# A recurrent-attention and SoLU kernel: an earlier opening, and two output banks copied out by ScalarE with the down products in another order

## The chip, the cores and the metric

One core of one Trainium2 chip. The metric is the device time of one execution in microseconds (us). All executions quoted are of the fast state (none is over 1.5% above the fastest of its kernel); a kernel is quoted by its median and by the spread of its runs. Each profile shows one execution, which is one of the runs listed (for the kernel before a further one, of 383.67 us); its span leaves out about 1.8 us that the run's own time contains (383.67 against 381.9 for the kernel before, 381.39 against 379.6 for the changed one). A *profile* here is the record of that execution, instruction by instruction; each experiment has one, so what one profile shows is one reading.

## The reference

```python
# attention: q, k, v, alpha are (4 batches, 8 heads, 768 tokens, 48), fp32
for t in range(S):
    state = alpha[:, :, t, :, None] * state + einsum('bhd,bhe->bhde', k[:, :, t], v[:, :, t])
    y[:, :, t] = einsum('bhd,bhde->bhe', q[:, :, t], state)
x = y.transpose(0, 2, 1, 3).reshape(3072, 384)

# SoLU MLP: w_in 384 x 1024, w_out 1024 x 384, both arrive as float64
h = x @ w_in
solu = h * softmax(h)
ln = (solu - mean(solu)) / sqrt(var(solu) + 1e-6) * g_ln
out = ln @ w_out
```

## The kernel before: the parts that matter

The recurrence is done in chunks of 128 tokens: running products of alpha (VectorE scans, backward and forward), scaled queries and keys, a masked score matrix for inside the chunk, and a state for what came before. A *group* is one chunk of all four batches, 512 tokens; there are six, 0 to 5. The MLP of group g runs beside the attention of group g+1. Two stretches are written out by hand: the **opening** (attention of group 0, with the float64 weights being unpacked by VectorE in `bits`) and the **turn** from the MLP of group 0 to that of group 1.

Some names of the profile's lines: `an` is alpha as loaded, `aT` alpha transposed and its forward running products, `hT` the backward ones, `kT` the keys, `qe` and `qv` the scaled queries, `a` the scores, `sT` the masked scores, `y` what attention reads out, `o` an output bank. In the MLP, *up* is x times w_in with the result `h`, `e` is its exp, the *product* is h times e on VectorE, and *down* is the matmul with w_out; d_ff is done in eight slices, so group 0 has eight products.

```python
def masked(half, batches=range(B)):              # VectorE: scores out of their bank, times the mask
    for b in batches:
        nc.vector.tensor_tensor(out=sT[:, b, half*NP : half*NP + NP], in0=masks[half][b],
                                in1=mask..., op=mult)

def down(n, half, part=slice(0, HF)):            # TensorE: 128 tokens n, half of the 8 slices of d_ff
    if half == 0 and part.start == 0:
        d["o"] = ps_o.tile([P, 512], FP, tag="o")    # an output bank; there are two
    for f in ...: nc.tensor.matmul(d["o"][:, 0:DM+1], lhsT=u_of(g, f)..., rhs=w_out[:, f], ...)

def finish(n):                                   # layer norm's mean and scale, then the store
    nc.vector.tensor_copy(out=s[:, 0:1], in_=d["o"][:, DM:DM+1])
    ... two more small VectorE instructions ...
    if g == 0:
        o = work.tile([P, DM], FP, name="o_mean")
        nc.vector.scalar_tensor_tensor(out=o, in0=mean_sb, scalar=s[:, 0:1], in1=d["o"][:, 0:DM], ...)
    nc.gpsimd.tensor_tensor(out=r, ..., op=pow)
    nc.scalar.activation(out=o_sb, in_=o, func=Copy, scale=r)
    nc.sync.dma_start(out=out[...], in_=o_sb)

# the opening
warm(18)                                         # 18 small matmuls, each recorded as two, to wake TensorE
turned(an, ...)                                  # alpha, transposed on TensorE
for i in range(3):
    nc.scalar.copy(out=aT[...], in_=t[i]); scan_back(0, i)
...
turned(qn, ends_of(qn), t)                       # queries
warm(2, ps_a, "a1")
for i in (2, 0, 1): ...                          # queries times aT
scores(0, 0); scores(0, 1, t); read_begin()
masked(0); masked(1)
bits(0)                                          # unpacks the first part of w_in
...
# the turn
mean(0); down(0, 1); mean(1); in_range(5); in_range(6); down(1, 1)
...
scan_on(1, 2); qe = tq[2] * aT; apart()
finish(0)
... two more scans and products, qv ...
down(2, 0); scores(1, 0)
finish(1)
alpha_over(1); load(alpha, an, 2)                # ScalarE's overflow test, then the next alpha
masked(0); down(2, 1); scores(1, 1); masked(1)
finish(2); alpha_T(2); read_begin()
... down(3, 0) in two parts, with the reads of the state ...
alpha_over(2); load(alpha, an, 3)
for i in range(3): scan_back(2, i)
keys_T(2); keys(2); load(k, kn, 3)
scan_on(2, 2); scan_on(2, 0)
read_values(1); down(3, 1); finish(3)
```

Of the kernel before, what the change touches and what calls it, by code (L numbers as in the profile page):

```python
# [16 lines left out]
P = 128  # L17
# [15 lines left out]
def fast_path(ctx, tc, q, k, v, alpha, moe_w_in, moe_w_out, moe_g_ln, out):  # L33
# [150 lines left out]
    def load_v_first(slot):  # L184
        x = slots[slot].rearrange("p (n d) -> p n d", d=D)
        y = vn.rearrange("p b h d -> p (b h) d")
        xi, yi = (z.rearrange("p (n i) d -> p i n d", i=2) for z in (x, y))
        nc.sync.dma_start(out=x, in_=v[:, :, 0:P].rearrange("b h p d -> p (b h) d"))
        for i in range(2):
            nc.gpsimd.tensor_copy(out=yi[:, i, :, all_of[i]], in_=xi[:, i])  # L190

# [299 lines left out]
    def down(n, half, part=slice(0, HF)):  # L491
# [4 lines left out]
        for f in range(half * HF + part.start, half * HF + part.stop):  # L496
# [2 lines left out]
                stop=(f == FC - 1), skip_group_check=True,  # L499
            )  # L500

    def finish(n):
        g, b = divmod(n, B)
        d = st[n]
        s, o = sums[:, n], d["o"][:, 0:DM]
        t0 = b * S + g * P
        if g == G - 1:
            o_sb = work.tile([P, DM], FP, name="o_sb")
            r = gr[g]["r"][:, b : b + 1]
            nc.scalar.activation(out=o_sb, in_=o, func=AF.Copy, scale=r)  # L510
            nc.scalar.dma_start(out=out[t0 : t0 + P, :], in_=o_sb)
            d.clear()
            return
        nc.vector.tensor_copy(out=s[:, 0:1], in_=d["o"][:, DM : DM + 1])
        t = small.tile([P, 1], FP, name="t")
        nc.vector.scalar_tensor_tensor(
            out=t, in0=s[:, 0:1], scalar=-1.0 / DFF, in1=s[:, 0:1], op0=ALU.mult, op1=ALU.mult
        )
        nc.vector.tensor_tensor(out=s[:, 3:4], in0=t, in1=gr[g]["s"][:, b : b + 1], op=ALU.add)  # L519
        if g == 0:  # L520

            o = work.tile([P, DM], FP, name="o_mean")
            nc.vector.scalar_tensor_tensor(  # L523
                out=o, in0=mean_sb, scalar=s[:, 0:1], in1=d["o"][:, 0:DM], op0=ALU.mult, op1=ALU.add
            )
        r = small.tile([P, 1], FP, name="r")
        nc.gpsimd.tensor_tensor(out=r, in0=s[:, 3:4], in1=mhalf, op=ALU.pow)  # L527
        o_sb = work.tile([P, DM], FP, name="o_sb")
        nc.scalar.activation(out=o_sb, in_=o, func=AF.Copy, scale=r)  # L529
        nc.sync.dma_start(out=out[t0 : t0 + P, :], in_=o_sb)  # L530
        d.clear()
# [83 lines left out]
    def mean(half):  # L615


        m = ps_h.tile([P, 512], FP, tag="h", name="sums")[:, 0:DM]
        if half == 0:
            for f in range(FC):  # L620
                r = quarter(f % 4)
                nc.tensor.matmul(
                    m[r], lhsT=ones[:, 0:32], rhs=w_out[:, f, 0:DM], start=f < 4, stop=f >= FC - 4,
                    tile_position=(0, r.start), skip_group_check=True,
                )
            made["m"] = work.tile([P, DM], FP, name="o_mean")
            nc.scalar.mul(out=made["m"], in_=m, mul=-1.0 / (32 * DFF))
        else:
            nc.tensor.matmul(m, lhsT=ones, rhs=made["m"], start=True, stop=True)
            nc.scalar.copy(out=mean_sb, in_=m)  # L630
# [33 lines left out]
        return [pool.tile([P, NP, P], FP, tag=tag, name=f"{name}{i}") for i, (pool, tag) in enumerate(where)]  # L664


    warm(18)
    t = three("tp_a", [(ps_a, "a0"), (ps_a, "a1"), (ps_a, "a2")])
    turned(an, ends_of(an), t)
    for i in range(3):  # L670
# [8 lines left out]
        nc.vector.tensor_tensor(out=kT[:, part], in0=t[i], in1=hk[:, part], op=ALU.mult)  # L679
    scan_on(0, 0)  # L680
    t = three("tp_q", [(ps_o, "o"), (ps_o, "o"), (ps_a, "a0")])
    turned(qn, ends_of(qn), t)

    warm(2, ps_a, "a1")
    for i in (2, 0, 1):
        if i == 1:
            scan_on(0, i)
# [7 lines left out]
    t = [x.tile([P, NP, P], FP, tag=n, name="a_" + n) for x, n in ((ps_h, "h"), (ps_o, "o")) for _ in range(2)]  # L695
    scores(0, 1, t)
    read_begin()
    masked(0)
    masked(1)
    bits(0)  # L700
    read_values(0)
# [51 lines left out]
    for i in range(3):  # L753
        scan_back(1, i)
        part = slice(NP * i, NP * i + NP)
        nc.vector.tensor_tensor(out=kT[:, part], in0=tk[i], in1=hk[:, part], op=ALU.mult)
    mean(0)
    down(0, 1)
    mean(1)
    in_range(5)  # L760
    in_range(6)
    down(1, 1)
    tq += three("tp_q2", [(ps_h, "h")])
    turned(qn, ends_q, tq, range(H, NB))
    load(q, qn, 2)
    keys_back(1, three("tp", [(ps_a, "a2"), (ps_a, "a3"), (ps_h, "h")]))
    scan_on(1, 2)
    nc.vector.tensor_tensor(out=qe, in0=tq[2], in1=aT[:, H:NB, 1:SW], op=ALU.mult)
    apart()
    finish(0)  # L770
    decay(1)
    in_range(7)
    for i in range(2):
        scan_on(1, i)
        part = slice(NP * i, NP * i + NP)
        nc.vector.tensor_tensor(out=qv[:, part], in0=tq[i], in1=aT[:, part, 1:SW], op=ALU.mult)
    down(2, 0)
    scores(1, 0)
    finish(1)
    alpha_over(1)  # L780
    load(alpha, an, 2)
    masked(0)
    down(2, 1)
    scores(1, 1)
    masked(1)
    finish(2)
    alpha_T(2)
    read_begin()
    for batches, part in (((0, 1), slice(0, HF // 2)), ((2, 3), slice(HF // 2, HF))):
        down(3, 0, part)  # L790
        for n in range(len(parts)):
            read_state(n, batches)
    alpha_over(2)
    load(alpha, an, 3)
    for i in range(3):
        scan_back(2, i)
    keys_T(2)
    keys(2)
    load(k, kn, 3)
    scan_on(2, 2)  # L800
    scan_on(2, 0)
    read_values(1)
    down(3, 1)
    finish(3)


# [6 lines left out]
    )  # L813
    first = dict(
        head={3: "keys_back", 5: "masked0", 6: "masked1"},
        behind={0: "states v", 1: "on1", 2: "lasts firsts", 3: "apart", 5: "decay", 7: "alpha back"},
        tail={4: "scores0", 5: "scores1", 6: "begin read0 read1"},
        middle={7: "read2 read3 values"},
    )
# [581 lines left out]
```

## Time and profile before

| | median of 3 runs, us | lowest | highest |
|---|---|---|---|
| before | 384.48 | 383.99 | 386.02 |

The head of the page of the kernel before: busy time of each engine, its share of the span, and its instructions.

```profile
span 381.9 us, 10525 instructions
PE 367.1 (96%) x4665; PEld 221.5 (58%) x4665; DVE 245.4 (64%) x381; ACT 144.6 (38%) x258; POOL 125.0 (33%) x132
```

TensorE (PE) is busy for 96% of the span. Only the remaining 14.8 us of the span are there to be won without removing matmuls, and the prediction below shows where they lie.

### The profile page before, as it was taken

Reading aid. Unit: us, or ns where it says so; the run is one execution under the profiler, and the core shown is the slowest. Engines: PE = TensorE matmul, PEld = TensorE weight load, DVE = VectorE, ACT = ScalarE, POOL = GpSimd, SP = SyncE. Lnnn points to the kernel's source line nnn. Section 1 sums busy time; section 2 is a strip of 40 time slices with the busy share of each in tenths; the row PEclk is TensorE's granted clock in tenths of the full one; section 3 lists DMA queues with packets and bytes.
Section 4 is the critical chain, followed back from the end, with each engine's and each line's share of the span. In section 5 each row is a group of like instructions: output and inputs, shape, how many; then the busy total and the mean of one; then the engine's idle time right before and its main releaser. Section 6 shows DMA issues by size and latency. Waiting matters only on the chain.

```text
span 381.9 us, 10525 instructions
## 1 busy us (share of the span) xinstructions
PE 367.1 (96%) x4665; PEld 221.5 (58%) x4665; DVE 245.4 (64%) x381; ACT 144.6 (38%) x258; POOL 125.0 (33%) x132
## 2 busy tenths in 40 slices
PE   8889999879899999999999999999999999999995
PEld 8675355547655666555576555575555675555552
DVE  0999879996989866893565884665875411554410
ACT  2628774384526244124252225351224131233111
POOL 5010000041055990544621553630562520333210
PEclk9999999999999999999999999999999999999999
DMA  9993989304457100961000960001500000000011
GB/s 183 164 330 95 222 270 164 85 21 101 110 115 118 40 4 4 186 143 44 22 3 27 203 145 21 23 12 37 81 0 22 22 24 2 21 21 21 22 44 49
DMA packets 65510, 30.78 MB, mean 81 GB/s; under 512 B 47016, under 2 KB 63664, under 8 KB 65456
## 3 DMA queue, kind: packets, MB, share of 16 engines
q1 hardware_dynamic: 64432, 29.10, 34.4%
q10 hardware_dynamic: 1024, 0.92, 0.7%
q8 instruction: 38, 0.62, 0.7%
q14 instruction: 16, 0.13, 0.1%
HBM read 25.30 MB, written 4.72 MB: 79 GB/s over the span
## 4 chain that ended last, share of the span: by engine, by line
PE 69%; DVE 16%; ACT 6%; DMA 3%; issue 3%; SPq 2%; POOL 0%; ACTq 0%; DVEq 0%
PE o L497 28%; PE h L386 23%; PE y L312 8%; PE a L278 5%; DVE aT L219 3%; DVE room L401 2%; SPq L153 2%; DMA qn<-in_q_dram 2%; DVE hT L219 2%; DVE sT L289 1%; ACT sq L576 1%; DVE aT L194 1%; DMA an<-in_alpha_dram 1%; PE kv L361 1%; DVE top L592 1%
## 5 line engine op out<-in xcount | busy, mean ns | idle before, releaser
L497 PE MATMUL o<-w_out,room 128*128 128x385 f32 x384 | 133.7, 492 | 2.4 <-DVE o_mean L523 2.4
L386 PE MATMUL h<-x,w_in 128*128 128x512 f32 x288 | 132.2, 599 | 0.2 <-DVE g_col L613 0.2
L497 PEld LDWEIGHTS o<-w_out,room 128*128 128x128 f32 x384 | 71.5, 190 | 58.3 <-issue 16.3
L386 PEld LDWEIGHTS h<-x,w_in 128*128 128x128 f32 x288 | 53.1, 190 | 58.8 <-issue 48.5
L401 DVE TENSOR_TENSOR room<-h,e 128x512 f32<-128x512 f32 x40 | 27.6, 689 | 82.1 <-ACT e L400 82.1
L400 ACT ACTIVATE e<-h 128x512 f32<-128x512 f32 x40 | 23.9, 597 | 108.2 <-PE h L386 108.2
L527 POOL TENSOR_TENSOR r<-sums,mhalf 128x1 f32<-128x1 f32 x20 | 14.3, 713 | 137.7 <-DVE sums L519 137.7
L417 POOL TENSOR_TENSOR p<-p,e 128x512 f32<-128x512 f32 x30 | 41.8, 1392 | 15.7 <-ACT e L400 15.7
L402 ACT ACTIVATE u<-room 128x512 f32<-128x512 f32 x40 | 25.2, 630 | 35.1 <-DVE room L401 35.1
L289 DVE TENSOR_TENSOR sT<-a,mask 128x512 f32<-128x512 f32 x44 | 27.3, 683 | 9.2 <-PE a L278 9.0
L219 DVE TENSOR_TENSOR_SCAN hT<-aT,unit 128x516 f32<-128x516 f32 x18 | 23.2, 1355 | 8.3 <-ACT aT L671 8.3
L240 POOL TENSOR_TENSOR kT<-kT,hT 128x1024 f32<-128x1024 f32 (+1 forms) x8 | 14.2, 1798 | 42.9 <-DVE kT L194 42.9
L219 DVE TENSOR_TENSOR_SCAN aT<-aT,seed 128x516 f32<-128x516 f32 x18 | 27.2, 1540 | 0.2
L417 DVE TENSOR_TENSOR p<-p,u 128x512 f32<-128x512 f32 x30 | 23.0, 765 | 6.5 <-ACT u L402 6.5
L278 PEld LDWEIGHTS a<-qv,kT 32*128 32x128 f32 x704 | 22.0, 187 | 8.6 <-issue 2.9
L278 PE MATMUL a<-qv,kT 32*128 32x128 f32 x704 | 25.0, 279 | 1.6 <-DVE qv L689 0.8
L312 PE MATMUL y<-sT,vn 128*32 128x128 f32 x768 | 23.6, 274 | 2.6 <-issue 1.5
L312 PEld LDWEIGHTS y<-sT,vn 128*32 128x32 f32 x768 | 20.9, 110 | 4.8 <-issue 3.4
L211 ACT ACTIVATE sq<-an,mone 128x1536 uint8<-128x1536 f32 x12 | 18.8, 1571 | 0.2
L312 PE MATMUL y<-qv,state 32*32 32x128 f32 x960 | 16.8, 277 | 0.3 <-issue 0.3
L312 PEld LDWEIGHTS y<-qv,state 32*32 32x32 f32 x960 | 12.1, 103 | 7.5 <-issue 5.4
L529 ACT ACTIVATE o_sb<-o,r 128x384 f32<-128x384 f32 x16 | 9.3, 581 | 18.7 <-POOL r L527 18.7
(140 smaller groups left out, 366.5 us busy)
## 6 DMA issues: line engine op xcount, KB each, us to landing
an<-in_alpha_dram SPq DMA_DIRECT2D x20, 192.0 KB, 4.1
vn<-in_v_dram SPq DMA_DIRECT2D x10, 384.0 KB, 5.6
out_dram<-o_sb SPq DMA_DIRECT2D x20, 192.0 KB, 1.9
room<-in_moe_w_in_dram SPq DMA_DIRECT2D x6, 512.0 KB, 8.7
room<-in_moe_w_out_dram SPq DMA_DIRECT2D x8, 384.0 KB, 4.0
kn<-in_k_dram SPq DMA_DIRECT2D x16, 192.0 KB, 4.3
qn<-in_q_dram SPq DMA_DIRECT2D x16, 192.0 KB, 3.8
kn<-in_k_dram SPq DMA_DIRECT2D x4, 384.0 KB, 5.7
```

The costliest lines, as they stand in the source:

```text
L211: nc.scalar.activation(out=sq, in_=x, func=AF.Relu, scale=sign, bias=mone, accum_out=over[:, g, i : i + 1])
L219: nc.vector.tensor_tensor_scan(out=o, data0=a, data1=s, initial=1.0, op0=ALU.mult, op1=ALU.add)
L278: nc.tensor.matmul(a[b][:, i], lhsT=kT[quarter(b), kb], rhs=qv[quarter(b), qb], start=kb == h, stop=kb != h, tile_position=(32 * b, 0), sk ...
L289: nc.vector.tensor_tensor(out=sT[:, b, half * NP : half * NP + NP], in0=a[b], in1=mask[:, None, :].to_broadcast([P, NP, P]), op=ALU.mult,)
L312: nc.tensor.matmul(y_bank(b)[quarter(r), a], lhsT=lhsT, rhs=rhs, start=(b, r) not in begun, stop=stop, tile_position=(row, 32 * r), skip_g ...
L386: nc.tensor.matmul(h, lhsT=w_in[:, a, f * P : (f + 1) * P], rhs=d["x"][:, a].rearrange("p b t -> p (b t)"), start=(a == 0), stop=(a == KC ...
L400: nc.scalar.activation(out=e, in_=h, func=AF.Exp)
L401: nc.vector.tensor_tensor(out=u, in0=h, in1=e, op=ALU.mult)
L402: nc.scalar.activation(out=u2, in_=u, func=AF.Square)
L417: eng.tensor_tensor(out=p, in0=d[0][i] if f == 1 else p, in1=d[f][i], op=ALU.add)
L497: nc.tensor.matmul(d["o"][:, 0 : DM + 1], lhsT=u_of(g, f)[:, b * P : b * P + P], rhs=w_out[:, f], start=(f == 0), stop=(f == FC - 1), skip ...
L527: nc.gpsimd.tensor_tensor(out=r, in0=s[:, 3:4], in1=mhalf, op=ALU.pow)
```

## The change

The intent: let the opening's chain (alpha, scans, queries, scores, masks) start earlier and relieve VectorE of two of its masks; in the turn, let ScalarE empty the two output banks so that TensorE need not wait for `finish`, move `finish` from VectorE's path into a gap, and ask for the next alpha earlier.

```diff
 # load_v_first: one load in two
-        nc.sync.dma_start(out=x, in_=v[:, :, 0:P]...)
+        for b in range(0, B, 2):
+            nc.sync.dma_start(out=x[:, H*b : H*b + 2*H], in_=v[b : b + 2, :, 0:P]...)
+    def moved(n):
+        o = work.tile([P, DM + 1], FP, name="o_mean")
+        nc.scalar.copy(out=o, in_=st[n]["o"][:, 0 : DM + 1])
+        st[n].update(o=o, moved=True)
 # the opening
-    warm(18)
+    nc.scalar.copy(out=small.tile([P, 1], FP, name="t"), in_=mhalf)   # activation tables now
+    warm(16)
-    turned(qn, ends_of(qn), t)
-    warm(2, ps_a, "a1")
+    turned(qn, ends_of(qn), t, [*range(NP), *range(H, NB), *range(NP, H)])
+    warm(1, ps_a, "a1")
-    masked(0)
+    for b in (2, 3):
+        s = sT[:, b, 0:NP]
+        nc.scalar.copy(out=s, in_=masks[0][b])
+        nc.gpsimd.tensor_tensor(out=s, in0=s, in1=mask..., op=ALU.mult)
+    masked(0, range(2))
     masked(1)
 # the turn
+    down(0, 1, slice(0, 2))
     mean(0)
-    down(0, 1)
+    down(0, 1, slice(2, HF))
+    moved(0)
     mean(1)
     in_range(5)
-    in_range(6)
     down(1, 1)
+    moved(1)
 ...                                          # in_range(6) comes a little later
-    finish(0)                                # from behind apart()
 ...
     down(2, 0)
+    down(2, 1)
     scores(1, 0)
-    finish(1)
     alpha_over(1)
     load(alpha, an, 2)
     masked(0)
-    down(2, 1)
+    finish(0)
+    finish(1)
+    down(3, 0)
     scores(1, 1)
     masked(1)
 ...
-        down(3, 0, part)                     # among the reads of the state
+        down(3, 1, part)
-    alpha_over(2)
-    load(alpha, an, 3)
 ...
     scan_on(2, 2)
-    scan_on(2, 0)
     read_values(1)
-    down(3, 1)
+    alpha_over(2)
+    load(alpha, an, 3)
+    down(3, 1, slice(3, HF))
     finish(3)
 # group 1's schedule: the scan taken out comes back behind slice 1
-        behind={..., 1: "on1", ...}
+        behind={..., 1: "on0 on1", ...}
```

More of the change, by code (lines that the diff above doesn't have):

```diff
@@ L187, in load_v_first @@
         xi, yi = (z.rearrange("p (n i) d -> p i n d", i=2) for z in (x, y))
-        nc.sync.dma_start(out=x, in_=v[:, :, 0:P].rearrange("b h p d -> p (b h) d"))
+        for b in range(0, B, 2):
+            nc.sync.dma_start(
+                out=x[:, H * b : H * b + 2 * H], in_=v[b : b + 2, :, 0:P].rearrange("b h p d -> p (b h) d")
+            )
         for i in range(2):
@@ L520, in finish @@
         if g == 0:
-            o = work.tile([P, DM], FP, name="o_mean")
+            if not d.get("moved"):
+                o = work.tile([P, DM + 1], FP, name="o_mean")[:, 0:DM]
             nc.vector.scalar_tensor_tensor(
@@ L625, in mean @@
                 )
-            made["m"] = work.tile([P, DM], FP, name="o_mean")
+            made["m"] = work.tile([P, DM + 1], FP, name="o_mean")[:, 0:DM]
             nc.scalar.mul(out=made["m"], in_=m, mul=-1.0 / (32 * DFF))
@@ L697, in fast_path @@
     read_begin()
-    masked(0)
+    for b in (2, 3):
+        s = sT[:, b, 0:NP]
+        nc.scalar.copy(out=s, in_=masks[0][b])
+        nc.gpsimd.tensor_tensor(out=s, in0=s, in1=mask[:, None, :].to_broadcast([P, NP, P]), op=ALU.mult)
+    masked(0, range(2))
     masked(1)
@@ L765, in fast_path @@
     load(q, qn, 2)
+    in_range(6)
     keys_back(1, three("tp", [(ps_a, "a2"), (ps_a, "a3"), (ps_h, "h")]))
@@ L788, in fast_path @@
     read_begin()
-    for batches, part in (((0, 1), slice(0, HF // 2)), ((2, 3), slice(HF // 2, HF))):
-        down(3, 0, part)
+    for batches, part in (((0, 1), slice(0, 2)), ((2, 3), slice(2, 3))):
+        down(3, 1, part)
         for n in range(len(parts)):
             read_state(n, batches)
-    alpha_over(2)
-    load(alpha, an, 3)
     for i in range(3):
@@ L815, in fast_path @@
         head={3: "keys_back", 5: "masked0", 6: "masked1"},
-        behind={0: "states v", 1: "on1", 2: "lasts firsts", 3: "apart", 5: "decay", 7: "alpha back"},
+        behind={0: "states v", 1: "on0 on1", 2: "lasts firsts", 3: "apart", 5: "decay", 7: "alpha back"},
         tail={4: "scores0", 5: "scores1", 6: "begin read0 read1"},
```

## The prediction

> **What bounds the kernel now.** I read the page's slices and chain first, then the table of stretches, then the chain in order of time, then each engine's timeline in the first 135 us. The chain of work that ended last gives TensorE 69% of the span and VectorE 16%:
>
> ```profile
> PE 69%; DVE 16%; ACT 6%; DMA 3%; issue 3%; SPq 2%; POOL 0%; ACTq 0%; DVEq 0%
> ```
>
> The chain in order of time shows where that 16% lies: before 130 us it runs mostly through VectorE, ScalarE and loads; from 130.03 us on it is TensorE alone until the last eviction at 377 us. The table of stretches says the same by busy time (columns: length, busy us and instructions of PE, PEld, DVE, ACT, POOL, then clock, DMA share, GB/s):
>
> ```profile
> 10.00:31.00 21.00, 17.32 (x478) 14.96 (x471) 19.86 (x28) 9.55 (x18) 1.65 (x3) 1.00 0.84 221
> 72.00:82.00 10.00, 7.71 (x61) 4.85 (x59) 9.62 (x16) 6.86 (x15) 0.50 (x1) 1.00 0.18 43
> 132.00:382.00 250.00, 245.27 (x2823) 142.85 (x2822) 137.00 (x232) 75.99 (x131) 94.72 (x94) 1.00 0.21 46
> ```
>
> The change removes no matmul from the last stretch, so all it can do is bring the moment at which TensorE stops waiting, 130 us, forward. The kernel has two places where that could begin: the opening (to 31 us) and the turn from chunk group 0 to group 2 (80 to 130 us).
>
> **The opening ends at a load.** VectorE's timeline:
>
> ```profile
> 24.86 1.28 DVE L289 TENSOR_TENSOR sT<-a_o,mask 128x512 f32<-128x512 f32 x2
> 26.18 0.95 DVE L589 TENSOR_SCALAR top<-room 128x768 uint32<-128x768 uint32 x1
> 30.63 0.16 DVE L613 TENSOR_SCALAR g_col<-tp_g 128x8 f32<-128x8 f32 x1
> ```
>
> The masks end at 26.14 and the unpacking of w_in (L589) follows without a gap; the first "up" matmul starts at 30.85, when that unpacking and g_col are done. It looks as if faster masks would bring all this forward. But the unpacking also waits for the first three w_in loads. The view of the loads' issue line, narrowed to the third one:
>
> ```profile
> L559 SPq DMA_DIRECT2D room<-in_moe_w_in_dram x1: 430/430/430, 18.9 to 18.9; - x1
> DMA to landing us min/median/max: 7.1/7.1/7.1
> ```
>
> Issued at 18.9 and landed 7.1 later, at 26.0 us. So the data came 0.14 us before the masks ended: a second limit right behind the first.
>
> **The turn** is a chain on VectorE with idle gaps (idle time before an instruction and its releaser in brackets):
>
> ```profile
> 85.60 0.15 DVE L514 COPY sums<-o 128x1 f32<-128x1 f32 x1
> 86.29 0.61 DVE L523 SCALAR_TENSOR_TENSOR o_mean<-mean_sb,sums,o 128x384 f32<-128x384 f32 x1
> 87.65 2.48 DVE L289 TENSOR_TENSOR sT<-a,mask 128x512 f32<-128x512 f32 x4 [0.76 <-PE a L278]
> 92.61 2.48 DVE L289 TENSOR_TENSOR sT<-a,mask 128x512 f32<-128x512 f32 x4 [2.47 <-PE a L278]
> ...
> 96.72 2.10 DVE L194 STREAM_TRANSPOSE aT<-an 128x1024 f32<-128x1024 f32 x1 [0.65 <-DMA an<-in_alpha_dram]
> ...
> 112.80 0.69 DVE L401 TENSOR_TENSOR room<-h,e 128x512 f32<-128x512 f32 x1 [1.26 <-ACT e L400]
> ```
>
> 0.76 + 2.47 + 0.65 + 1.26 = 5.1 us in which the engine on the path stood still. On TensorE in the same time the one long wait is for an output bank that only finish(0) frees:
>
> ```profile
> 82.09 2.83 PE L497 MATMUL o<-w_out,room 128*128 128x385 f32 x8 [2.38 <-DVE o_mean L523]
> ```
>
> and alpha for group 2 is late because its issue follows an overflow test (L211) that ScalarE only starts at 87.78, after finish(1)'s scaling.
>
> **What the Trainium skill says.** "ScalarE: Activation LUTs", What ACT_TABLE_LOAD costs: a table load is about 1283 ns whatever the set. The trace has one of 1.28 us at 6.80, just when alpha lands; agreed. "PSUM — Partial Sum Buffer", Specifications: GpSimd neither reads nor writes PSUM, hence the two masks need a ScalarE copy first; no run so far shows more. "SBUF — State Buffer", SBUF: two separate sides: a VectorE instruction with two SBUF inputs and a GpSimd one that reads SBUF exclude each other. The trace agrees: the scans (L219) take 1.23 us alone and 2.24 each at 106 us, beside GpSimd's kT products.
>
> **Part by part, opening.** Table load moved ahead (a dummy copy): ScalarE can evict from 7.4 instead of 8.1. Two warm-up pairs fewer: 4 x 0.18 = 0.7 us, TensorE starts on alpha at 6.8 instead of 7.49. Both bring the scans forward 0.7. Then the queries: their load lands at 14.86 as before, the bank needed first is now turned second, so it is ready 0.9 us earlier (32 of 96 small matmuls, 2.84/3): qe at 16.8 instead of 17.74. Masks: VectorE drops 2 x 0.62 = 1.24; ScalarE adds 2 x 0.58, GpSimd 2 x about 1.25 (its 128x512 products of L251), done near 24, in time for the last batch. So the masks end near 24.6, 1.5 us earlier, and x and the key transposes about 2 us earlier. But the unpacking cannot start before 26.0 plus 0.1: its own gain is 0.1. Splitting the v load moves the same bytes through the same queue ahead of w_in, so I give the landing no change. What survives is ScalarE's: its range tests (L576/L577, 4 us) delayed the first exp to 35.24 though h was there at 33.6; they now end near 32.5. After that the loop waits on TensorE's own pace (h of the second slice at 37.7, its exp at 38.00). **Gain carried past 58 us: 0.25.**
>
> **Part by part, turn** (before in brackets). From 58 to 81 us VectorE never stops, so moving two down matmuls ahead of mean(0) fills TensorE's 0.98 us wait and gains nothing on the path. qe ends 80.7 (80.96). finish(0), 1.0 us, is gone from here; scan, product, scan, product take 3.84: 84.55 (85.70). Scores 1.95 later: first mask at 86.5 (87.65), four masks 2.46: 88.95. TensorE, freed of the 2.38 wait by moved(0) (ScalarE, about 0.5 us, idle there), has done both halves of down(2) by then and puts down(3,0), 2.8, between: 89.35; second scores 2.07: 91.35. Beneath them VectorE does finish(0) and finish(1), 2 x 1.0, to 90.95, so the 2.47 gap shrinks to 0.4. Second masks end 93.85, finish(2) 94.85. Alpha: spread queries end 82.1, range test 1.95, overflow test 3.36, load 5.5 as now: lands 93.0, no longer waited for. So alpha's transposition starts at 94.9 (96.72): **-1.8**.
>
> From there 9.37 to the second scan's start and 2.24 for it: 106.5. finish(3) now follows one scan instead of two; its sum is there at 107.0 (111.0), but GpSimd's kT product, in order before its power, ends 107.7 (109.48); power 0.55, scaling 0.6, exp 0.5: first L401 of group 1 at 109.4 (112.80), -3.4. The overflow test moved behind the x copies ends near 105.6, harmless. The scan taken out there comes back at slice 1: 1.2 to 1.7 us. So L401 of slice 2 is at 115.7 (117.73): **-2.0**. The rest of that loop is the same on VectorE, masked(0) at 125.6 (127.59), and TensorE is then never idle again. 384.48 - 2.0 = 382.5; because scans escape some contention in the new place, I put the middle at 382.3.
>
> **The rivals.** (1) The opening's gain comes through whole: if the w_in loads land about 1.5 us earlier, everything shifts 1.5 and the time is near 381. For: VectorE is 95% busy there and the chain passes through its masks. Against: 26.0 us of landing. (2) The turn is bound by TensorE, not VectorE: then filling its 2.38 wait and the wait near 103 would count, up to 4 us off, 380.5. For: TensorE is busy 14.51 of 15 us from 82 to 97; against: VectorE's order forces the scans. (3) The finish work moved, not removed, collides: if finish(0) and finish(1) delay the second masks by 1 us, or alpha still comes late, gain under 1, 383.7. (4) GpSimd or ScalarE holds up the last batch's read: they have about 2 us of room before the unpacking ends, so only a GpSimd mask of over 3 us would hurt.
>
> **Range and chances.** Main line 382.5 with 1 us either way from scan contention and finish, rival 1 or 2 (three in ten) to 380.5, rival 3 (two in ten) to 383.8; the runs before spread from 383.99 to 386.02. I say 382.3, 380.3 to 383.9. Two per cent is 7.7 us, more than all of VectorE's gaps in the turn: faster 0.03, same 0.96, slower 0.01.
>
> **What would show it.** Right: an idle gap of 1 to 1.5 us before the first L589-type unpacking, ended by the w_in load; first up matmul still within 0.3 of 30.8; no wait of down(2,0) for finish; no wait for alpha at 95; first product of group 1 about 3 us earlier but slice 2's only about 2; TensorE solid from about 128. Wrong: w_in landing clearly before or after 26, a mask on GpSimd ending after 27, scans over 2 us in slice 1, or new waits on TensorE after 130 us.

## The result, and the profile after

| same rounds | median, us | lowest | highest | runs |
|---|---|---|---|---|
| before | 384.9 | 383.99 | 386.02 | 4 |
| changed | 381.6 | 381.39 | 381.79 | 4 |

The ratio is 0.9913, with a 95% interval of 0.9884 to 0.9942: within 2%, so "same" by that measure, though the gain of about 3 us is real. (A ratio here is the mean time of one kernel's fast runs over that of the other's of the same rounds, so not quite the ratio of the medians quoted.)

The head of the changed kernel's page, and its chain of work by engine:

```profile
span 379.6 us, 10523 instructions
PE 366.9 (97%) x4659; PEld 220.9 (58%) x4659; DVE 243.8 (64%) x379; ACT 146.8 (39%) x263; POOL 128.4 (34%) x134
...
PE 76%; DVE 15%; DMA 3%; ACT 2%; issue 2%; SPq 1%; POOL 0%; DVEq 0%
```

TensorE does the same work (366.9 against 367.1 us). VectorE lost 1.6 us to ScalarE (+2.2) and GpSimd (+3.4). The span fell by 2.3 us, so what went is waiting. TensorE's part of the chain grew from 69 to 76%.

**Where TensorE stops waiting.** The chain in order of time (columns: start, length, engine and line), at the scores after which nothing but TensorE is on it. Before, then after:

```profile
130.03 2.05 PE a L278 x58
```

```profile
127.44 2.05 PE a L281 x58
```

2.59 us earlier. The last output matmul ends 2.41 us earlier (377.38, now 374.97): that is nearly the whole difference of the spans, so everything was won before 130 us.

**The opening after**, VectorE's timeline (start, length, operation; in brackets the idle time before it and what ended it):

```profile
22.58 1.29 DVE L292 TENSOR_TENSOR sT<-a_h,mask 128x512 f32<-128x512 f32 x2 [0.55 <-PE a_o L281]
23.78 1.28 DVE L292 TENSOR_TENSOR sT<-a_o,mask 128x512 f32<-128x512 f32 x2
25.44 0.95 DVE L599 TENSOR_SCALAR top<-room 128x768 uint32<-128x768 uint32 x1 [0.38 <-DMA room<-in_moe_w_in_dram]
...
29.88 0.16 DVE L623 TENSOR_SCALAR g_col<-tp_g 128x8 f32<-128x8 f32 x1
```

The masks now end at 25.06 instead of 26.14 and unpacking waits 0.38 us for the w_in load. VectorE has two masks (1.24 us) fewer to do, but 0.55 us of that go into a new wait for the second half of the scores, which TensorE is still computing. The new wait is the predicted one, but the load is there at 25.3, not at 26.0. The eighth product of group 0 (L401, now L404), the last step before the turn, starts at 57.32 instead of 57.93: the opening gave **0.61 us** in this pair of profiles.

**The turn after**, the same view:

```profile
86.08 2.48 DVE L292 TENSOR_TENSOR sT<-a,mask 128x512 f32<-128x512 f32 x4 [1.97 <-PE a L281]
...
91.04 2.48 DVE L292 TENSOR_TENSOR sT<-a,mask 128x512 f32<-128x512 f32 x4 [0.51 <-PE a L281]
...
94.42 2.04 DVE L197 STREAM_TRANSPOSE aT<-an 128x1024 f32<-128x1024 f32 x1
...
103.74 2.39 DVE L222 TENSOR_TENSOR_SCAN aT<-aT,seed 128x516 f32<-128x516 f32 x1
...
109.12 0.69 DVE L404 TENSOR_TENSOR room<-h,e 128x512 f32<-128x512 f32 x1 [1.27 <-ACT e L403]
...
111.61 2.96 DVE L222 TENSOR_TENSOR_SCAN aT<-aT,seed 128x516 f32<-128x516 f32 x2
...
115.07 0.68 DVE L404 TENSOR_TENSOR room<-h,e 128x512 f32<-128x512 f32 x1
```

The 2.47 us gap before the second masks is 0.51, the 0.65 us wait for alpha is gone, the 1.26 us gap before the first product of group 1 stands. The masks of group 2 start at 124.92 (127.51): counted from the eighth product of group 0, the turn took 69.58 us and takes 67.60, **1.98 us** less. 0.61 + 1.98 = 2.59.

What binds inside the turn changed as well. The chain in order of time, before (first masks' scores, a down product, part of the second scores, then the issue and the flight of alpha's load):

```profile
85.74 2.06 PE a L278 x62
87.80 2.79 PE o L497 x8
90.59 0.55 PE a L278 x13
...
92.54 4.16 DMA an<-in_alpha_dram
96.72 2.10 DVE aT L194
```

and after:

```profile
78.88 5.19 PE o L500 x16
84.07 2.17 PE a L281 x61
86.23 2.79 PE o L500 x8
89.02 2.03 PE a L281 x64
91.06 2.47 DVE sT L292 x4
```

Before, the turn's middle hung on alpha's arrival at 96.7; now it hangs on TensorE without a break from 78.88 to 91.06. VectorE's last qv product ends in the same moment as the 16 down matmuls (84.1), so the two engines are level there.

### The profile page after: what moved, and what is told of

Its sections match the earlier page's. It is cut to its first block, busy times and chain, and to the rows that moved or that the text cites. A ratio compares the mean times of both kernels' runs of the same rounds, so it can differ in the third digit from the quotient of the medians.

```text
span 379.6 us, 10523 instructions
## 1 busy us (share of the span) xinstructions
PE 366.9 (97%) x4659; PEld 220.9 (58%) x4659; DVE 243.8 (64%) x379; ACT 146.8 (39%) x263; POOL 128.4 (34%) x134
## 4 chain that ended last, share of the span: by engine, by line
PE 76%; DVE 15%; DMA 3%; ACT 2%; issue 2%; SPq 1%; POOL 0%; DVEq 0%
PE o L500 30%; PE h L389 26%; PE y L315 8%; PE a L281 5%; DVE hT L222 3%; PE warm L445 2%; DVE sT L292 1%; PE kv L364 1%; DMA an<-in_alpha_dram 1%; DMA out_dram<-o_sb 1%; DVE aT L222 1%; PE tp L300 1%; DVE aT L197 1%; DVE room L404 1%; PE rows L455 1%
## 5 line engine op out<-in xcount | busy, mean ns | idle before, releaser
L404 DVE TENSOR_TENSOR room<-h,e 128x512 f32<-128x512 f32 x40 | 27.6, 689 | 82.1 <-ACT e L403 82.0
L292 DVE TENSOR_TENSOR sT<-a,mask 128x512 f32<-128x512 f32 x42 | 26.1, 682 | 8.3 <-PE a L281 8.2
L263 POOL TENSOR_TENSOR state<-state,hT 128x192 f32<-128x192 f32 x20 | 11.3, 581 | 53.0 <-DVE hT L222 53.0
L222 DVE TENSOR_TENSOR_SCAN aT<-aT,seed 128x516 f32<-128x516 f32 x18 | 26.3, 1494 | 0.2
L315 PE MATMUL y<-sT,vn 128*32 128x128 f32 x768 | 23.6, 274 | 2.4 <-issue 2.0
```

The lines of the kernel that those rows point to most:

```text
L222: nc.vector.tensor_tensor_scan(out=o, data0=a, data1=s, initial=1.0, op0=ALU.mult, op1=ALU.add)
L292: nc.vector.tensor_tensor(out=sT[:, b, half * NP : half * NP + NP], in0=a[b], in1=mask[:, None, :].to_broadcast([P, NP, P]), op=ALU.mult,)
L315: nc.tensor.matmul(y_bank(b)[quarter(r), a], lhsT=lhsT, rhs=rhs, start=(b, r) not in begun, stop=stop, tile_position=(row, 32 * r), skip_g ...
L404: nc.vector.tensor_tensor(out=u, in0=h, in1=e, op=ALU.mult)
```

## The experiments

Twelve experiments in three jobs, five to seven runs each, all fast and all correct. The kernel before ran 11 times in each job: medians 384.39, 384.37 and 384.01, lowest 383.55, 383.6 and 383.39, highest 386.52, 389.14 and 387.47.

| job | kernel | median, us | lowest to highest | ratio to before [95%] |
|---|---|---|---|---|
| 1 | opening alone | 382.75 | 382.44 to 383.65 | 0.9960 [0.9936, 0.9984] |
| 1 | turn alone | 382.70 | 381.62 to 385.17 | 0.9955 [0.9922, 0.9988] |
| 1 | copies of the banks alone | 385.66 | 384.32 to 387.62 | 1.0036 [1.0002, 1.0071] |
| 1 | changed, v in one load | 381.26 | 380.68 to 384.35 | 0.9927 [0.9894, 0.9961] |
| 2 | changed, all masks on VectorE | 381.15 | 380.79 to 382.56 | 0.9898 [0.9854, 0.9942] |
| 2 | changed, old start | 382.09 | 381.59 to 383.19 | 0.9923 [0.9878, 0.9968] |
| 2 | changed, scan where it was | 381.20 | 380.75 to 382.42 | 0.9904 [0.9859, 0.9949] |
| 2 | changed, finish(3) later | 380.02 | 379.89 to 382.69 | 0.9871 [0.9827, 0.9914] |
| 3 | changed, once more | 381.03 | 380.50 to 382.28 | 0.9911 [0.9877, 0.9944] |
| 3 | both gaps closed | 380.32 | 380.12 to 380.99 | 0.9901 [0.9864, 0.9938] |
| 3 | both gaps closed, one wait filled | 380.67 | 380.03 to 381.84 | 0.9899 [0.9866, 0.9932] |
| 3 | changed, eight matmuls more | 383.36 | 381.36 to 385.61 | 0.9987 [0.9946, 1.0028] |

And what their profiles show, in us: the start of the first unpacking, of the eighth product of group 0, and the turn (from there to the masks of group 2).

| kernel | unpacking | eighth product | turn | span |
|---|---|---|---|---|
| before | 26.18 | 57.93 | 69.58 | 381.9 |
| changed | 25.44 | 57.32 | 67.60 | 379.6 |
| opening alone | 24.78 | 56.62 | 69.66 | 380.6 |
| turn alone | 25.89 | 59.93 * | 67.66 | 383.2 |
| copies alone | 25.90 | 57.56 | 70.45 | 382.9 |
| v in one load | 25.14 | 56.84 | 67.76 | 379.4 |
| all masks on VectorE | 24.91 | 58.62 * | 67.61 | 380.8 |
| old start | 25.63 | 57.97 | 67.81 | 381.4 |
| scan where it was | 25.14 | 56.98 | 67.92 | 379.4 |
| finish(3) later | 25.25 | 58.78 * | 66.98 | 380.9 |
| changed, once more | 25.29 | 56.96 | 67.76 | 380.5 |
| both gaps | 24.88 | 56.97 | 66.70 | 378.4 |
| both gaps, filled | 24.84 | 58.02 | 66.98 | 380.0 |
| eight matmuls more | 24.98 | 57.28 | 67.83 | 379.6 |

\* In these profiles the clock granted to TensorE between 26 and 29 us was 0.52 to 0.57 of full speed instead of 1.00, while it read group 0. That costs about 1.5 to 2 us, falls on old and new openings alike, and must be left out when openings are compared.

### 1 and 2: each half of the change alone

```diff
 opening alone = before, with these hunks of the change and no others
+  v load in two; nc.scalar.copy(t <- mhalf); warm(16); queries in the new order; warm(1)
+  batches 2, 3 of masked(0): ScalarE copy, GpSimd product

 turn alone = before, with all the other hunks
+  moved(); down(0,1) in two; finish(0), finish(1) behind masked(0); down(2,1), down(3,0) ahead
+  alpha_over/load ahead; scan_on(2, 0) to slice 1 of group 1
```

> The kernel before with the opening's part of the change alone (table load ahead, shorter warm-up, queries in another order, v in two loads, two masks over ScalarE and GpSimd). Theory (opening and turn add up; the opening is held by the landing of the first three w_in loads): first unpacking of w_in at 25.4 to 25.5 us, first L401-type product at 35.3, span 0.6 us below the kernel before, 0.4 to 0.9. Rival (the opening gains 1.5 us as the earlier masks would give): span 1.3 us or more below. Rival (the gain is all in the turn): under 0.2 us.

> The kernel before with the turn's part alone (banks emptied by ScalarE, downs, finishes and tests in another order, one scan moved into group 1). Theory: span 1.7 us below the kernel before (1.4 to 2.1), first masks of the turn about 1 us earlier than 87.65, no wait for alpha, and with the opening's 0.6 it makes the sum of the whole change. Rival (the parts need each other): clearly under 1.2 or, with the opening alone, not adding up to 2.3.

The two are worth the same by their medians: 384.39 - 382.75 = 1.64 and 384.39 - 382.70 = 1.69; together 3.3, which is what the whole change gives. Their lowest runs, less touched by scatter, give 1.1 (383.55 - 382.44) and 1.9 (383.55 - 381.62). The traces split it the same way: the turn is 69.66 with the new opening alone and 67.66 with the new turn alone, and the eighth product comes 1.3 us earlier with the new opening. **The turn was sized right; the opening was not**: 0.4 to 0.9 had been expected, and its span is 1.2 us below that of before (381.88, now 380.65), near the rival's 1.3. VectorE's timeline of the opening alone:

```profile
24.78 0.95 DVE L592 TENSOR_SCALAR top<-room 128x768 uint32<-128x768 uint32 x1 [0.19 <-DMA room<-in_moe_w_in_dram]
```

The w_in load let unpacking begin at 24.8 here. Reading the same third w_in load (its issue plus its time to landing) in all fourteen profiles gives between 23.6 and 26.1; the kernel before, whose single profile the prediction rested on, had the latest of them all. With the turn alone, whose opening is that of before to the letter, it landed at 24.0, and with the copies alone, where that also holds, at 25.0.

### 3: the bank copies alone

This is the test of rival 2: TensorE's 2.38 us wait for an output bank is taken away; apart from that only `in_range(6)`, a range test of ScalarE, moves a little.

```diff
     down(0, 1)
+    moved(0)
     mean(1)
     in_range(5)
-    in_range(6)
     down(1, 1)
+    moved(1)
+    in_range(6)
```

> The kernel before plus the two ScalarE copies of the first two chunks out of their banks, finishes and downs where they were. Theory (VectorE's order binds the turn, not the bank): TensorE's wait of 2.38 us before down(2,0) goes, but VectorE's first masks stay within 0.3 us of 87.65 and the span within 0.3 us of the kernel before. Rival 2 of the prediction (TensorE binds the turn): the masks and the span come 1 to 2 us earlier.

385.66: **slower by about 1 us** (within 0.3 had been expected), with 1.000 just outside the interval. The bank wait is gone from the trace, but VectorE's path is untouched, so TensorE only gets to its next wait sooner. TensorE's timeline:

```profile
83.48 0.48 PE L278 MATMUL a<-qv,kT 32*128 32x128 f32 x2 [1.56 <-DVE qv L785]
85.35 2.83 PE L278 MATMUL a<-qv,kT 32*128 32x128 f32 x62 [1.39 <-DVE sums L520]
88.11 3.71 PE L497 MATMUL o<-w_out,room 128*128 128x385 f32 x8
```

It waits 1.56 + 1.39 us instead. And then the same work takes longer: 62 score matmuls 2.83 us where the kernel before has 2.06 (85.74 in its timeline), 8 down matmuls 3.71 where it has 2.83. The table of stretches (length, busy us and count of PE, PEld, DVE, ACT, POOL, clock, DMA share, GB/s) of the copies alone shows what goes with it:

```profile
84.00:88.00 4.00, 2.65 (x62) 2.54 (x62) 2.59 (x7) 1.15 (x4) 3.17 (x5) 0.81 0.03 9
88.00:92.00 4.00, 4.00 (x19) 2.18 (x20) 2.30 (x4) 3.15 (x4) 0.00 (x0) 0.77 0.13 49
```

The granted clock fell to 0.81 and 0.77; in the kernel before both stretches are at 1.00. Rival 2 is refuted: the bank wait was slack behind VectorE, and removing it alone only gathers TensorE's idle time into another place, followed, in this profile, by a slower clock. The mean clock of every run, which the record gives, says the same: the three runs at 0.996 to 0.998 took 384.32 to 384.73 us, as long as the kernel before, and the three at 0.990 and 0.991 took 386.58 to 387.62. So the copies gain nothing by themselves, and the microsecond goes with the clock.

### 4: the v load in one piece again

Its theory was that splitting the v load is what brings w_in in earlier.

```diff
-        for b in range(0, B, 2):
-            nc.sync.dma_start(out=x[:, H*b : H*b + 2*H], in_=v[b : b + 2, ...]...)
+        nc.sync.dma_start(out=x, in_=v[:, :, 0:P]...)
```

> The changed kernel with v loaded in one transfer again. Theory (the split lets the w_in loads be issued earlier; in the changed kernel the third of them landed 0.7 us earlier than before): the third w_in load lands at about 26.0 again, the first unpacking starts there, span 0.5 us above the changed kernel's 379.6. Rival (the split is neutral and the 0.7 us is scatter of the queue): unpacking at 25.4 and span within 0.2 us of 379.6.

381.26, no different from the changed kernel (381.6 and 381.03), and w_in landed at 25.0. The theory falls: **the split is neutral**, and the landing moves by itself from one profile to the next.

### 5: all masks on VectorE again

```diff
-    for b in (2, 3):
-        ... ScalarE copy, GpSimd product ...
-    masked(0, range(2))
+    masked(0)
     masked(1)
```

> The changed kernel with all eight opening masks on VectorE again. Theory (masks and w_in landing are two limits close to each other; in the changed kernel the load is the later one, by 0.4 us): the masks end 1.2 us later, at about 26.3 us, the first unpacking follows without a wait for the load, and the span is 0.5 to 1.0 us above the changed kernel's 379.6. Rival (the load alone is the limit, masks are hidden): unpacking within 0.2 us of 25.4, span within 0.2.

381.15. The masks end at 25.00, the load has landed at 24.6, unpacking starts at 24.91 without a wait. The masks had been expected to end at 26.3; they end only 0.3 to 0.4 us later than in its two neighbours of the same job with the new start (24.72 and 24.56), because VectorE, with two masks fewer, waits about 0.55 us for the second scores (22.58 above). **Taking two masks off VectorE is worth nothing that can be measured**: what it takes away goes partly into that wait and partly into the one for the w_in load.

### 6: the old start

```diff
-    nc.scalar.copy(out=small.tile([P, 1], FP, name="t"), in_=mhalf)
-    warm(16)
+    warm(18)
 ...
-    warm(1, ps_a, "a1")
+    warm(2, ps_a, "a1")
```

> The changed kernel with 18 and 2 warm-up pairs and the table load where it was. Theory of the prediction (both bring the scans 0.7 us forward): first scan back at 10.0, span 0.5 to 0.7 us above 379.6. Rival (seen in the two profiles: the first scan starts at 9.33 in both, so neither was on the path): first scan within 0.1 of 9.33 in most runs or scattered by TensorE's warm-up alone, span within 0.3 us.

382.09, which is 0.9 more than its neighbours of the same job (381.15 and 381.20); by lowest runs 0.8. Its eighth product starts at 57.97, as late as with the old opening at full clock (57.93 before, 57.56 with the copies alone). With the new start at full clock it comes at 56.6 to 57.3 in seven of eight profiles, and at 58.02 in the other, "both gaps, filled" (experiment 12 says why); so one profile alone would not decide it. By the runs **the start carries most of what the opening gives**: 0.8 to 0.9 of 1.1 to 1.6 us. TensorE's first rows, before, changed, and changed with the old start:

```profile
1.04 6.52 PE L442 MATMUL warm<-ones 128*128 128x128 f32 x36 [1.04 <-DVE w_out L661]
```

```profile
1.04 6.52 PE L445 MATMUL warm<-ones 128*128 128x128 f32 x32 [1.04 <-DVE w_out L671]
```

```profile
1.04 7.17 PE L445 MATMUL warm<-ones 128*128 128x128 f32 x36 [1.04 <-DVE w_out L671]
```

These three lines also hold a trap. 36 matmuls took 6.52 us in one profile and 7.17 in another, because the moment at which their pace doubles differs from execution to execution: from one start to the next it is 213 ns first and 112 ns later, and the change comes after 22 of them in the kernel before, 26 in the changed one and 28 with the old start (read from the packed traces; the clock column shows 1.00 throughout). In the pair before and changed it hid the whole gain: alpha's first transposes start at 7.49 in both, and the first scan at 9.33 in both. In the other profiles with the new start the first scan begins at 8.40 to 9.19, with the old start at 9.19 to 9.97. ScalarE's half of the start is in the trace as intended, changed kernel:

```profile
2.81 1.28 ACT L678 ACT_TABLE_LOAD   x1 [2.81 <-issue]
...
6.80 0.62 ACT L162 COPY ends<-an 128x512 f32<-128x512 f32 x1 [2.50 <-DMA an<-in_alpha_dram]
```

The first copy starts as alpha lands, 1.29 us sooner than the 8.09 of before.

### 7: the scan back in its old place

```diff
     scan_on(2, 2)
+    scan_on(2, 0)
 ...
-        behind={..., 1: "on0 on1", ...}
+        behind={..., 1: "on1", ...}
```

> The changed kernel with the second scan of group 2 back in front of finish(3). Theory (it delays the power and with it the first product of group 1 by one scan, of which slice 1 gives the scan back): first L404-type product of group 1 2.0 to 2.4 us later than 109.12 against the same opening, that of slice 2 and the masks 0.8 to 1.2 us later, span 0.8 to 1.2 above 379.6. Rival (the order is neutral since VectorE does the same work): under 0.3.

381.20, and a turn of 67.92 against 67.60 and 67.76: **neutral**, 0.3 us at most, where 0.8 to 1.2 had been expected. (The prediction itself had given this move only 0.2: its gain of 1.8 at alpha's transposition became 2.0 at the third product.) VectorE's timeline with the scan back in its place:

```profile
103.53 4.48 DVE L222 TENSOR_TENSOR_SCAN aT<-aT,seed 128x516 f32<-128x516 f32 x2
...
108.09 0.16 DVE L525 SCALAR_TENSOR_TENSOR t<-sums 128x1 f32<-128x1 f32 x1
...
112.72 1.83 DVE L222 TENSOR_TENSOR_SCAN aT<-aT,seed 128x516 f32<-128x516 f32 x1
```

Its scans take 4.48 + 1.83 = 6.31 us; those of the changed kernel, one here and two later, 2.39 + 2.96 = 5.35. That is 0.96 us less, and yet the third product, counted from the start of the first of these scans, comes after 11.52 us with the scan back and after 11.33 in the changed kernel (103.53 to 115.05, 103.74 to 115.07). The rest went into the second small instruction of finish(3), 0.16 us above, which took 0.92 in the changed kernel:

```profile
106.22 0.92 DVE L525 SCALAR_TENSOR_TENSOR t<-sums 128x1 f32<-128x1 f32 x1
```

It ends at 107.14. GpSimd's timeline in the same profile:

```profile
102.86 4.25 POOL L243 TENSOR_TENSOR kT<-kT,hT 128x1024 f32<-128x1024 f32 x2 [8.19 <-DVE kT L197]
```

The key products end at 107.11. In all seven profiles that have this order of the turn (one scan, then finish(3)) this instruction takes 0.91 to 0.92 us and ends within 0.03 us of GpSimd's product; where a second scan or the first product of group 1 stands before it, it takes 0.16. So what VectorE has to do with two inputs in SBUF beside this product waits for GpSimd, be it the scan or an instruction on a single column; taking the scan away only made the next one wait.

### 8: finish(3) behind the first product of group 1

The wait that stands in the changed kernel is 1.27 us before the first product of group 1, because exp stands behind finish(3)'s scaling on ScalarE.

```diff
     down(3, 1, slice(3, HF))
-    finish(3)
 ...
-        after = None
+        after = 3 if g == 1 else None      # finish(3) behind the first up and product of group 1
```

> The changed kernel with finish(3) behind the first up step of group 1 instead of in front of it. Theory (VectorE binds from 94 to 127 us and its one gap, 1.27 us before the first product of group 1, comes from the power and the scaling of finish(3) ahead of the exp): the gap goes, products, masks and span come 1.0 to 1.4 us earlier: span about 378.4. Rival (TensorE or GpSimd's query products bind this stretch): gap gone but span within 0.4 us of 379.6.

380.02, **the best version**: 1.1 to 1.2 us under its neighbours of the same job, by lowest runs 0.9. The turn is 66.98. The product does more than come first: its h lies in PSUM, where TensorE wrote it, and not in SBUF, and beside GpSimd's key products (104.38 to 108.64 in this profile) it starts at 107.76 and takes its usual 0.69 us, where the finish in its place had to wait. Its profiled run was the slowest of its seven (382.69), with the clock at 0.53 while reading group 0.

### 9 to 11: the changed kernel once more, both gaps closed, and one wait filled

```diff
 both gaps closed = finish(3) later, and:
-    down(3, 0)
+    down(3, 0, slice(0, 3))
     scores(1, 1)
+    down(3, 0, slice(3, HF))
     masked(1)

 filled = both gaps closed, and ahead of the scores of group 2:
+            if g == 1 and s == 4:
+                warm(6)
```

> The changed kernel itself once more, beside the kernel before on the chip of the next three runs. Median 381.2 to 381.7, ratio to before about 0.992; in its profile the opening ends (product of the eighth slice of group 0) between 56.6 and 57.4 us if TensorE's clock stays up during the reading of group 0, and at about 58.7 if it drops, and the stretch from there to the masks of group 2 takes 67.6 to 67.8 us either way.

> The changed kernel with finish(3) behind the first up step and the last quarter of down(3,0) behind the second scores of the turn. Theory (VectorE's gaps of 0.5 and 1.27 us in the turn are on the path): second masks of the turn follow finish(1) without a gap, the stretch from the eighth product of group 0 to the masks of group 2 takes 66.5 us or less (67.6 in the changed kernel, 67.0 with finish(3) late alone), median 1.2 to 1.9 us below the changed kernel's of the same job. Rival (what is left is bound elsewhere): not below the 380.0 of finish(3) late alone.

> The same with six idle matmuls in TensorE's wait before the first scores of group 2. Theory (TensorE's clock drops after such waits in some executions and the spread of the times comes from there): the wait becomes busy time, the times scatter less than those of the run without and the median is equal or up to 0.5 us lower. Rival (the six matmuls are work on the path): 0.3 to 0.8 us slower.

Changed 381.03 (381.2 to 381.7 had been expected), both gaps 380.32, filled 380.67. With both gaps closed, VectorE's timeline:

```profile
105.70 0.69 DVE L404 TENSOR_TENSOR room<-h,e 128x512 f32<-128x512 f32 x1 [0.36 <-ACT e L403]
...
109.74 0.69 DVE L404 TENSOR_TENSOR room<-h,e 128x512 f32<-128x512 f32 x1 [1.31 <-ACT e L403]
...
113.80 0.68 DVE L404 TENSOR_TENSOR room<-h,e 128x512 f32<-128x512 f32 x1
```

The second masks start with no gap at 90.19, the first product of group 1 starts at 105.70 instead of 108.85 (in the changed kernel of that job). But a new wait of 1.31 us for exp stands in front of the second product, and by the third the lead is 1.0 us (113.80 against 114.78). The whole turn is 66.70 against 67.76, 1.1 us less (finish(3) later alone had 66.98), just short of the 66.5 expected, and its profile has the shortest span of all, 378.4. The medians show 0.7, where 1.2 to 1.9 had been expected, and 380.32 is not below the 380.02 of finish(3) later, though the two ran in different jobs: the rival's sign. I take them for equal.

The filling was meant for the clock. In the profile of the changed kernel of this job TensorE waited 1.24 + 0.33 us ahead of the scores of group 2, and then:

```profile
121.00:124.00 3.00, 3.00 (x57) 2.70 (x58) 2.03 (x3) 1.65 (x3) 2.92 (x3) 0.69 0.74 150
124.00:127.00 3.00, 3.00 (x6) 1.05 (x5) 3.00 (x5) 0.00 (x0) 3.00 (x4) 0.74 0.00 0
```

(The clock is the third number from the end.) In the first profile of the very same kernel, after waits of 1.15 + 0.33 us, both stretches are at 1.00.

That slow stretch cost about 1.1 us: the masks of group 2 came 0.2 us earlier than in the first profile, and the span is 0.9 longer. Filling the wait removed it from the trace, but the runs are neither faster nor closer together (380.03 to 381.84): that cause of scatter isn't confirmed as a large one.

### 12: eight small matmuls more ahead of the queries

Reading group 0, TensorE stops once for something the profile calls "issue". The experiment shifts the count of instructions: `warm(8)` makes eight matmuls, each of them recorded as two.

```diff
     t = three("tp_q", [(ps_o, "o"), (ps_o, "o"), (ps_a, "a0")])
+    warm(8, ps_a, "a1")
     turned(qn, ends_of(qn), t, ...)
```

> The changed kernel with eight idle matmuls (16 TensorE instructions of each kind) in the wait for the queries, so that every later TensorE instruction has a number higher by 16. Theory (the wait in the reading of group 0 that the profile calls issue sits at a fixed instruction number, a wait for instructions): it comes after 11 recorded matmuls of the reading instead of 27 (21 with the old warm-up). Rival (it waits for data: masks, v or the w_in load): it stays after 27. Span within 0.7 us of the changed kernel's.

TensorE's timeline, changed kernel first, shifted second:

```profile
22.49 0.41 PE L315 MATMUL y<-sT,vn 128*32 128x128 f32 x4
23.32 1.07 PE L315 MATMUL y<-sT,vn 128*32 128x128 f32 x23 [0.42 <-DVE sT L292]
25.40 2.85 PE L315 MATMUL y<-sT,vn 128*32 128x128 f32 x96 [1.01 <-issue]
```

```profile
22.27 0.41 PE L315 MATMUL y<-sT,vn 128*32 128x128 f32 x4
23.10 0.63 PE L315 MATMUL y<-sT,vn 128*32 128x128 f32 x8 [0.42 <-DVE sT L292]
24.91 3.36 PE L315 MATMUL y<-sT,vn 128*32 128x128 f32 x114 [1.18 <-issue]
```

The stop came after 27 of the recorded matmuls and comes after 12 (11 had been expected). In every profile with the old warm-up, which has six recorded matmuls more, it comes after 21, six sooner than with the new one. Counted from the start of the program, 477 or 478 matmuls are recorded ahead of it in every one of the fourteen profiles; a later stop of this kind stands behind 1498 or 1499 in eleven of them. A stop that goes by the number of instructions issued, and not by data, is most likely a **wait for the instructions themselves**; the runs show the first half of this sentence, not what the fetching does.

The stop was 0.58 us in the kernel before, 1.01 in the changed one and 0.27 to 1.82 elsewhere. Mostly unpacking on VectorE runs beside it and sets the pace: in eight profiles the first up matmul follows the first unpacking by 4.66 to 4.68 us. But the longest stop decides: in "both gaps, filled" it lasted 1.82 us, the first up matmul came 5.72 us after the first unpacking, and the eighth product at 58.02 instead of 57.0. The runs of this kernel are slow and scattered (381.36 to 385.61), while the profiled run is the fastest of the six (381.36), so its profile cannot show the reason. The mean clocks on record go with the times: 1.000 in the two fastest runs, 0.988 to 0.997 in the other four; what lowers the clock stays open.

## Why the prediction was right, and where not

**Right in the whole.** It had 382.3 and about 2.2 us; the medians of the first rounds gave 381.6 and 3.3, the traces 2.3, the later job 3.0. The outcome to which it gave 0.96, "within 2%", came; that band is 7.7 us wide on either side and asks little. That the time fell 0.7 us below its middle fits the opening, which it had too small.

**Right: only the time before 130 us can give anything.** All of the shift is there at 127.44 us, and no part of TensorE's solid stretch got shorter.

**Right: the turn, step by step.** Each predicted start against the trace:

| step | before | predicted | after |
|---|---|---|---|
| first masks | 87.65 | 86.5 | 86.08 |
| second masks | 92.61 | 91.35 | 91.04 |
| alpha's transposition | 96.72 | 94.9 | 94.42 |
| end of the scan behind it | | 106.5 | 106.13 |
| first product, group 1 | 112.80 | 109.4 | 109.12 |
| third product, group 1 | 117.73 | 115.7 | 115.07 |
| masks, group 2 | 127.51 | 125.6 | 124.92 |

All are 0.3 to 0.7 us earlier than predicted, mostly the 0.36 us by which the opening gave more in this profile (0.61 against 0.25). The turn itself was put at 2.0 - 0.25 = 1.75 and is 1.98 by the traces of the pair, 1.9 by lowest runs and 1.7 by medians of the turn alone. Alpha is no longer waited for, and the first product of group 1 gains 3.7 us of which the third keeps 2.7 (3.4 and 2.0 were given). The scans put into slice 1 take 1.48 us each, inside the 1.2 to 1.7 given.

**Wrong: the size of the opening's term.** "Gain carried past 58 us: 0.25" was 0.6 in the pair of profiles, 1.1 by lowest runs and 1.6 by medians of the opening alone. The step that failed is "the unpacking cannot start before 26.0 plus 0.1: its own gain is 0.1", and behind it "I give the landing no change". 26.0 was one reading of a quantity that lies anywhere between 23.6 and 26.1 in fourteen profiles. With the old opening the masks bound (they end at 26.14, 25.97 and 25.98 in its three profiles), with the load 0.1, 2.0 and 1.0 us ahead of them; the room behind the masks was therefore about 1 us on average and not 0.14. Of the signs named in advance, two failed accordingly: the gap before unpacking was 0.38 us, not 1 to 1.5, and the first up matmul started at 30.11, not within 0.3 of 30.8. Two terms before that step were off in this pair as well. The shorter warm-up was to bring the scans 0.7 us forward (4 x 0.18 us); the first scan starts at 9.33 in both, and the four matmuls left out are of the fast ones at the end, 0.11 us each. And the masks, put at 24.6, end at 25.06, because VectorE waits 0.55 us for the second scores.

**Rival 1 was half right.** "Everything shifts 1.5 and the time is near 381" is near what was measured, and "the w_in loads land earlier" is what lets it pass. But its lever, the faster masks, gives nothing (experiment 5), nor does the split of the v load (4). The early start gives most of it (6). The order of the queries was not tried by itself; it takes away VectorE's wait before qe (0.42 us in the kernel before, none with the old start and the new order), so a share of the gain may be its own.

**Rival 2 is refuted as it was meant** (experiment 3). Yet after the change TensorE does carry the chain from 78.88 to 91.06 us, level with VectorE: a wait that is slack before a change can be the next bound after it. **Rival 3 and 4** did not come: finish(0) and finish(1) leave a gap of 0.51 before the second masks, the GpSimd masks hold nobody up.

**Not foreseen:** new waits of 1.15 + 0.33 us on TensorE ahead of the scores of group 2 (for GpSimd's and ScalarE's query products). At full clock they cost nothing, VectorE setting the pace there.

**Open.** By medians the change gives 3.0 to 3.3, by the traces at full clock 2.3 to 2.9. Single executions lie up to 5.5 us above the lowest of the same kernel and job. The profiles that fell on a slow one of their kernel (turn alone, all masks on VectorE, old start, finish(3) later, changed once more) show stretches of lower TensorE clock, and so does that of the copies alone, which did not; the one of both gaps filled, the slowest of its six, shows none, but the longest stop for instructions. The gain does not come from the clock: of the runs with a mean clock of 0.998 or more, the twelve of the kernel before have a median of 384.20 and the seven of the changed one 381.12, 3.1 us less. Why the traces show less than the runs stays open, and so does what sets the landing of w_in and what lowers the clock.

## What to carry to other kernels

A limit that lies 0.1 us behind another in one profile is not a limit until it has been read in several executions: the same load behind the same opening landed 2.1 us apart. Removing an engine's longest wait pays only where that engine's next work is not itself waiting for the chain; the bank copies alone gained nothing, and the same copies within a reordering that also freed VectorE and alpha's load gained nearly 2. After a change, look for what still stands in front of an in-order engine: moving one `finish` behind the exp that the path needed was worth another microsecond.

## What the Trainium skill lacked or had wrong

- **"TensorE: Matmul & The Clock Gate"**, Part 1, What's actually happening, and HAM oscillation: the clock is said to fall after an idle window of about 3.4 us, and the rule given is no idle gaps above that. Here it was lower in stretches after gaps of only 1.24 + 0.33 us (clock 0.69 and 0.74) and 1.56 + 1.39 us (0.81 and 0.77), and stayed at 1.00 in another execution of the same kernel after 1.15 + 0.33 us. Gaps well under 3.4 us are no guarantee. (The page's section "A second HAM failure mode" does tell of frequent short idle stretches, but gives no length for them.)
- **"Runtime: NRT & Kernel Launch"**, Instruction fetch mechanics, says that fetching is hidden by the pace of issue. Here TensorE stopped for 0.27 to 1.82 us behind 477 or 478 recorded matmuls in each of fourteen profiles, and sixteen more of them ahead of the reading of group 0 moved the stop from behind its 27th to behind its 12th. If that is the fetch (that it goes by the count of instructions is shown, what the fetching does is not), it is not always hidden.
- **No page** gives the scatter of a load's landing under a full queue: the third w_in load, in the same place in the order, landed between 23.6 and 26.1 us in fourteen profiles.
- **"SBUF — State Buffer"**, SBUF: two separate sides, says that a VectorE instruction with two SBUF inputs and a GpSimd one that reads SBUF exclude each other for a whole instruction; the runs agree. What it does not give is how small a victim may be: an instruction on one column took 0.92 us instead of 0.16 and ended 0.02 us after GpSimd's product.
